# One matmul per partition sum, another order of the first loads, and revised planner estimates, in a fused long-convolution and feed-forward kernel

## The chip, the core and the metric

The kernel runs on one core of a Trainium2 chip. A core has five engines with instruction streams of their own: TensorE (PE in the profile, PEld for its weight loads), VectorE (DVE), ScalarE (ACT), GpSimd (POOL) and SyncE (SP), which here only issues loads and stores. The metric is the device time of one execution in microseconds (us), lower is better; a kernel's time is the median of its runs.

## What is computed

```python
x  = A_q                                  # [1, 2048, 1024]
xn = layernorm(x)                         # over the last axis, eps 1e-5

# A: gated long convolution, channel by channel
k_shift = sum over t of k_pad[:, t:t+S] * shift_k[:, 3-t]     # 4 taps, causal
kv = k_shift * v
y  = irfft(rfft(pad(kv)) * rfft(pad(ssm_k)))[:S] + kv * ssm_D
A  = xn * y

# B: feed-forward, 1024 -> 3584 -> 1024
B  = silu(xn @ w1) @ w2

out = x + A + B
```

The inputs are float32. The kernel splits every operand of its large products into a high and a low float16 part and multiplies high by high, high by low and low by high, so each product of the algorithm is three matmuls. The scale factors for these parts are powers of two, which come from sums of squares over a whole operand.

## The kernel before

**An order written by a planner.** The kernel doesn't issue its instructions in the order of its text. Each piece of work is a generator ("stream") that yields operations (`Op`, line 81) with an engine, an estimated busy time, what is read and written, and a margin. `Order.run` (line 153) keeps a clock for each engine, takes the stream whose next operation could start earliest (less a bias that the stream has set), emits it, and moves the engine's clock on by the estimate. So an estimate doesn't only describe: it decides in which order the instructions of all five engines stand in the program. On the chip each engine then works through its own list in order and waits where data are missing. The estimates are in four helpers: `V` for VectorE (line 232), `A` for ScalarE (235), `T` for TensorE (238) and `L` for loads on SP's queue (241). Nearly all VectorE operations are recorded by lines 250 and 253 (`v_tt`, `v_stt`), nearly all of ScalarE by line 261 (`a_act`), and the loads and stores by line 243, so in the profile one goes by tile names.

**Rows of x.** x has 16 row tiles of 128 x 1024. `load_row` (370) loads one into a ring of four buffers, `xt`. `ln_rows` (376) takes rows in pairs: statistics on VectorE (`bn_stats`, two halves, line 394) or, for two later pairs, on ScalarE; a square root on ScalarE; a chain of six short VectorE instructions (410 to 415); and the normed row (426), written to a ring of eight buffers, `xn`. `transposes` (433) turns normed rows into column order on TensorE (line 447), through three PSUM tiles `ft`. `first_rows` (455) splits rows 0 to 3 into the operands A11 and A12; `x_rows` (518) makes the sums and differences of a Strassen-Winograd scheme for the rest.

**The first GEMM.** w1 is taken in 14 pairs of 128-column blocks. `load_pair` (579) loads one: the first two in four pieces each (tiles named `x` in the trace, whose space they borrow), the others in two pieces (`raw`). `scales_w1` (600) squares the pieces on ScalarE with a running total for each piece and partition, sums them with `norm`, and derives the scale; `factors_w1` (636) splits the blocks into the tiles `wo`. `feed_forward` (804) first computes four plain units (pairs 0 and 1 by rows 0 to 3, then by rows 4 to 7), then 12 units of seven products for the first half of the rows and 14 for the second; lines 748 to 750 are their matmuls. `evacuate` and `block` turn the results into hidden tiles `ht` (a ring of four) and store them to memory (`hs`).

**The sum over partitions.** `norm` (336) has columns of partial sums in `ss`, in one or two groups of `ns` columns. A product with a 128 x 128 matrix of ones puts the sum over all partitions into every partition: one matmul for each column, accumulated over a group's columns (line 349). Then a chain on VectorE rounds to a power of two (332, 333) and computes scales (618 to 622 for w1). `norm` is called 14 times for w1 (4 columns for the first two pairs, 2 for the others), and for each of the 8 channel groups of the convolution twice: in `gate` with 4 + 2 columns and in `result_scales` with 4; once more for w2 with one.

**The convolution and the second GEMM.** For each of 8 groups of 128 channels: the taps and the product with v on ScalarE and VectorE (`gate`, 988), transposes (1045), a first transform stage by matmuls with constants (1072 to 1074, tiles `ps`), butterflies and the complex product on VectorE (`forward`, `product`, `inverse`), a split into `zh` and `zl`, the inverse stage by matmuls (1276 to 1278, tiles `py`), and the gate with xn, `yt`, which is added to the output by DMAs on GpSimd's queue (247; two `yt` buffers). Between these stand the products of the first GEMM and, from about the middle of the run on, those of the second: `feed_forward` loads hidden tiles into `wo` and multiplies them by the split w2 (832 to 834), for 2 column halves x 16 row tiles x 28 blocks x 3 parts, 2688 matmuls. Their streams have a bias of zero, so they fill what the convolution leaves.

**The start.** `begin` (1313) issues row 0, the first w1 pair, rows 1 to 3 and the second pair; then `more_rows` and `more_pairs` go on side by side. The convolution's constants (`taps`, `cfw`, `civ`) follow the fourth pair's place in `more_pairs`. Line 1342 loads ScalarE's square-root table ahead of everything.

Of the kernel before, what the change touches and what calls it, by code (L numbers as in the profile page):

```python
# [17 lines left out]
AX = mybir.AxisListType  # L18
# [189 lines left out]
def h3_ffn_kernel(ctx, tc, x, kp, vs, fs, shift, dskip, w1, w2, cfwd, cinv, out):  # L208
# [26 lines left out]
    def A(f, o, ins, us=None, m=0.15):  # L235
        return Op("ACT", us or 1.03 * (0.12 + size(o) * 0.98e-3), 0.2, f, ins, [o], m)
# [19 lines left out]
    def a_act(o, i, func, scale=1.0, bias=None, total=None):  # L256
# [61 lines left out]
    xts_r = Ring(order, lnp, "xt", 4)  # L318
    xns_r = Ring(order, lnp, "xn", 8)
# [16 lines left out]
    def norm(ring, ss, ns, then, flags):  # L336
# [6 lines left out]
        cols = len(ns)  # L343

        def mm():
            for c, n in enumerate(ns):
                for a in range(n):
                    i = sum(ns[:c]) + a
                    nc.tensor.matmul(pt[:, c:c + 1], ones, ss[:, i:i + 1], start=(a == 0), stop=(a == n - 1))
# [20 lines left out]
    def load_row(t):  # L370
        yield xts_r.ready
        xts[t] = xts_r.tile([P, D])
# [3 lines left out]
    def ln_rows():  # L376
        for t0, n, on_act, bias in ((0, 2, 0, 0.2), (2, 2, 0, 0.17), (4, 2, 0, 0.13), (6, 2, 0, 0.12),
# [5 lines left out]
            for t in range(t0, t0 + n):  # L383
# [4 lines left out]
                else:  # L388
# [3 lines left out]
                    def stats(st=st, ag=ag, xt=xt, i=i):  # L392
                        for a in range(2):
                            nc.vector.bn_stats(st[:, a, :], xt[:, a * W:(a + 1) * W])
# [3 lines left out]
                    p = V(stats, m[:, 0, i], [xt], us=1.5)  # L398
# [17 lines left out]
            p = V(chain, rstd[:, q], [m[:, 3, :], m[:, 4, :], m[:, 0, :]], us=0.6)  # L416
            p.writes += [nmr[:, q], m[:, 5, :]]
            yield p
            for t in range(t0, t0 + n):
                yield xns_r.ready  # L420
                xns[t] = xns_r.tile([P, D], uses=4 if t < 4 else 2)
                xn, xt, i = xns[t][0], xts[t][0], slice(t - t0, t - t0 + 1)
                if on_act:
                    yield a_act(xn, xt, AF.Identity, rstd[:, t:t + 1], nmr[:, t:t + 1])
                else:
                    yield V(lambda: nc.vector.tensor_scalar(xn, xt, m[:, 0, i], rstd[:, t:t + 1], op0=ADD, op1=MUL),
# [970 lines left out]
```

## Time and profile before

| what | us |
|---|---|
| median of 3 runs | 1356.01 |
| lowest and highest run | 1355.55, 1360.4 |
| the profiled execution | 1360.99 |
| its span | 1358.9 |
| TensorE busy in it | 1301.7 |
| VectorE busy | 1184.0 |
| ScalarE busy | 689.2 |
| GpSimd busy | 99.4 |

The span runs from the first to the last instruction that the profiler saw. Busy time is the union of an engine's instructions. TensorE's matmuls are pipelined: a 128 x 512 matmul is shown with some 0.38 us, but the next one starts 0.215 us after it, so the distance of two starts is the cost of one, and a TensorE that is shown as busy is not for that reason at its full rate. In rows of the timeline the columns are start, duration, engine, line, operation, tiles written and read, shape and count, and in brackets the idle time before, with what ended it. In rows by line the numbers behind the bar are busy us and mean ns of one, and behind the next bar the idle time before them. In a table of stretches each engine has its busy time and, in brackets, its number of instructions, and the last three columns are the granted clock, the busy share of the DMA engines and GB/s.

### The profile page before, as it was taken

Reading aid. Unit: us, or ns where it says so; the run is one execution under the profiler, and the core shown is the slowest. Engines: PE = TensorE matmul, PEld = TensorE weight load, DVE = VectorE, ACT = ScalarE, POOL = GpSimd, SP = SyncE. Lnnn points to the kernel's source line nnn. Section 1 sums busy time; section 2 is a strip of 40 time slices with the busy share of each in tenths; the row PEclk is TensorE's granted clock in tenths of the full one; section 3 lists DMA queues with packets and bytes.
Section 4 is the critical chain, followed back from the end, with each engine's and each line's share of the span. In section 5 each row is a group of like instructions: output and inputs, shape, how many; then the busy total and the mean of one; then the engine's idle time right before and its main releaser. Section 6 shows DMA issues by size and latency. Waiting matters only on the chain.

```text
span 1358.9 us, 18422 instructions
## 1 busy us (share of the span) xinstructions
PE 1301.7 (96%) x6394; PEld 642.1 (47%) x6394; DVE 1184.0 (87%) x1856; ACT 689.2 (51%) x1211; POOL 99.4 (7%) x102
## 2 busy tenths in 40 slices
PE   6899999999999989999899999999999999999998
PEld 5544454444444444444444544545544454454443
DVE  6987999889899968999989999999999999999600
ACT  6879787878567665546533433423473252341200
POOL 0000000000000011000120120120110020021110
PEclk9899999999999998999999999999999999999999
DMA  8257588989899887758775485575596366355461
GB/s 310 78 168 228 185 286 292 328 286 394 289 315 328 280 249 200 227 156 261 214 173 157 112 197 148 122 187 143 124 292 177 97 150 185 91 125 127 112 128 16
DMA packets 206861, 269.69 MB, mean 198 GB/s; under 512 B 15400, under 2 KB 121904, under 8 KB 204336
## 3 DMA queue, kind: packets, MB, share of 16 engines
q1 hardware_dynamic: 184752, 251.73, 58.1%
q0 software_dynamic: 22016, 16.78, 10.2%
q8 instruction: 50, 0.82, 0.2%
q14 instruction: 43, 0.35, 0.1%
HBM read 192.96 MB, written 83.89 MB: 204 GB/s over the span
## 4 chain that ended last, share of the span: by engine, by line
PE 33%; issue 25%; DVE 22%; DMA 11%; ACT 5%; POOL 3%; SPq 0%; POOLq 0%; DVEq 0%; ACTq 0%
PE ff L750 8%; PE ff L749 8%; PE ff L748 8%; DVE spec L250 6%; POOL out L247 3%; DMA out<-yt 3%; DMA raw<-in_w 2%; DVE acc L253 2%; DMA kin<-in_kp 2%; DVE tmp L250 2%; PE ff L833 2%; PE ff L834 2%; PE ff L832 2%; DVE wo L253 1%; DVE x L253 1%
## 5 line engine op out<-in xcount | busy, mean ns | idle before, releaser
L833 PE MATMUL ff<-x,wo 128*128 128x512 f16 x896 | 342.3, 382 | 4.8 <-DVE x L253 4.8
L834 PE MATMUL ff<-x,wo 128*128 128x512 f16 x896 | 342.3, 382 | 0.0
L832 PE MATMUL ff<-x,wo 128*128 128x512 f16 x896 | 341.8, 381 | 0.0
L748 PE MATMUL ff<-x,wo 128*128 128x512 f16 (+1 forms) x808 | 306.4, 379 | 2.3 <-ACT wo L261 2.3
L750 PE MATMUL ff<-x,wo 128*128 128x512 f16 (+1 forms) x808 | 305.9, 379 | 2.1 <-DVE wo L253 2.1
L749 PE MATMUL ff<-x,wo 128*128 128x512 f16 (+1 forms) x808 | 305.7, 378 | 0.6 <-DVE x L253 0.6
L250 DVE TENSOR_TENSOR spec<-spec 128x512 f32<-128x512 f32 (+2 forms) x192 | 219.7, 1174 | 1.3
L834 PEld LDWEIGHTS <-wo 128*128 128x128 f16 x896 | 88.2, 98 | 112.9 <-issue 8.8
L832 PEld LDWEIGHTS <-wo 128*128 128x128 f16 x896 | 89.0, 99 | 100.8 <-issue 2.2
L833 PEld LDWEIGHTS <-wo 128*128 128x128 f16 x896 | 88.1, 98 | 101.2 <-issue 2.4
L750 PEld LDWEIGHTS <-wo 128*128 128x128 f16 x808 | 79.8, 99 | 98.9 <-DVE wo L253 4.7
L247 POOL DMA_DIRECT2D out<-yt x64 | 70.5, 1102 | 752.4 <-DMA w2n<-in_w 484.5
L748 PEld LDWEIGHTS <-wo 128*128 128x128 f16 x808 | 81.4, 101 | 89.7 <-ACT wo L261 2.5
L749 PEld LDWEIGHTS <-wo 128*128 128x128 f16 x808 | 80.0, 99 | 88.5 <-issue 1.9
L250 DVE TENSOR_TENSOR tmp<-spec 128x512 f32<-128x512 f32 (+1 forms) x112 | 100.7, 917 | 0.3
L253 DVE SCALAR_TENSOR_TENSOR ht<-hf,wsc,ht 128x512 f16<-128x512 f32 x112 | 83.2, 746 | 8.5 <-ACT ht L261 8.2
L261 ACT ACTIVATE xg<-xg,nmr,rstd 128x128 f32<-128x128 f32 x128 | 55.1, 484 | 65.9 <-DMA xg<-in_x 54.2
L261 ACT ACTIVATE ht<-hf,wsc 128x512 f16<-128x512 f32 x112 | 80.8, 721 | 3.4
L253 DVE SCALAR_TENSOR_TENSOR acc<-kin,taps,acc 128x512 f32<-128x512 f32 x96 | 71.7, 747 | 8.7 <-ACT acc L261 8.6
L261 ACT ACTIVATE hf<-hf,wsc 128x512 f32<-128x512 f32 x78 | 55.8, 715 | 40.5 <-DVE hf L250 40.4
L261 ACT ACTIVATE kin<-acc 128x512 f32<-128x512 f32 x32 | 20.1, 627 | 102.3 <-DVE acc L250 102.2
L261 ACT ACTIVATE v<-ff,invc 128x512 f32<-128x512 f32 x32 | 21.7, 677 | 94.3 <-PE ff L834 94.2
(152 smaller groups left out, 1834.9 us busy)
## 6 DMA issues: line engine op xcount, KB each, us to landing
wo<-hs SPq DMA_DIRECT2D x224, 256.0 KB, 3.1
hs<-ht SPq DMA_DIRECT2D x112, 256.0 KB, 3.8
ws<-wo SPq DMA_DIRECT2D x84, 256.0 KB, 4.6
wo<-ws SPq DMA_DIRECT2D x84, 256.0 KB, 4.2
w2n<-in_w SPq DMA_DIRECT2D x80, 256.0 KB, 5.4
raw<-in_w SPq DMA_DIRECT2D x28, 512.0 KB, 6.0
kin<-in_kp SPq DMA_DIRECT2D x32, 448.0 KB, 3.7
xt<-in_x SPq DMA_DIRECT2D x16, 512.0 KB, 4.8
```

Source lines behind the costliest of these rows:

```text
L247: return Op("POOL", 1.1, 4.0, lambda: nc.gpsimd.dma_start(o, i, accum_op=ADD), [i], [o], m, n)
L250: return V(lambda: nc.vector.tensor_tensor(o, a, b, op=op), o, [a, b], **k)
L253: return V(lambda: nc.vector.scalar_tensor_tensor(o, a, s, b, op0=op0, op1=op1), o, [a, b] + ([] if isinstance(s, float) else [s]), **k)
L261: nc.scalar.activation(o, i, func, scale=scale, **kw)
L748: nc.tensor.matmul(o, w[:, 0, k], xf[:, :, k, 0], start=first and k == 0, stop=False, **kw)
L749: nc.tensor.matmul(o, w[:, 0, k], xf[:, :, k, 1], start=False, stop=False, **kw)
L750: nc.tensor.matmul(o, w[:, 1, k], xf[:, :, k, 0], start=False, stop=last and k == KH - 1, **kw)
L832: nc.tensor.matmul(po, hx[:, jj, 0, :], wc[:, jj, 0, :], start=(j == 0), stop=False)
L833: nc.tensor.matmul(po, hx[:, jj, 0, :], wc[:, jj, 1, :], start=False, stop=False)
L834: nc.tensor.matmul(po, hx[:, jj, 1, :], wc[:, jj, 0, :], start=False, stop=(j == NF - 1))
```

## The change

```diff
     def A(f, o, ins, us=None, m=0.15):
-        return Op("ACT", us or 1.03 * (0.12 + size(o) * 0.98e-3), 0.2, f, ins, [o], m)
+        return Op("ACT", us or 1.02 * (0.16 + size(o) * 0.84e-3), 0.2, f, ins, [o], m)
...
-        return Op("SP", 0.07, 0.1, lambda: nc.sync.dma_start(o, i), [i], [o], m, n)
+        return Op("SP", 0.4, 0.1, lambda: nc.sync.dma_start(o, i), [i], [o], m, n)
...
         p = A(f, o, ins)
+        p.busy += 0.07 * (len(ins) - 1) - 0.06 * (i.space == bass.MemoryType.PSUM)
...
-    xts_r = Ring(order, lnp, "xt", 4)
-    xns_r = Ring(order, lnp, "xn", 8)
+    xts_r = Ring(order, lnp, "xt", 12)
...
-        cols = len(ns)
+        cols, n = len(ns), sum(ns)
 
         def mm():
-            for c, n in enumerate(ns):
-                for a in range(n):
-                    i = sum(ns[:c]) + a
-                    nc.tensor.matmul(pt[:, c:c + 1], ones, ss[:, i:i + 1], start=(a == 0), stop=(a == n - 1))
-
-        outs = []
+            nc.tensor.matmul(pt[:, 0:n], ones, ss, start=True, stop=True)
 
         def chain():
-            pow2(e[:, 0:cols], pt[:, 0:cols])
+            for c, m in enumerate(ns):
+                q = sum(ns[:c])
+                if m > 1:
+                    nc.vector.tensor_reduce(e[:, c:c + 1], pt[:, q:q + m], axis=AX.X, op=ADD)
+                else:
+                    nc.vector.tensor_copy(e[:, c:c + 1], pt[:, q:q + 1])
+            pow2(e[:, 0:cols], e[:, 0:cols])
             then(e[:, 0:cols])
 
-        yield T(mm, pt[:, 0:2], [ss], 0.12 * sum(ns), m=0.5)
-        p = V(chain, e, [pt[:, 0:2]], us=0.6)
+        yield T(mm, pt[:, 0:n], [ss], 0.25, m=0.5)
+        p = V(chain, e, [pt[:, 0:n]], us=1.1)
...
-        xts[t] = xts_r.tile([P, D])
+        xts[t] = xns[t] = xts_r.tile([P, D], uses=4 if t < 4 else 2)
...
-            p = V(chain, rstd[:, q], [m[:, 3, :], m[:, 4, :], m[:, 0, :]], us=0.6)
+            p = V(chain, rstd[:, q], [m[:, 3, :], m[:, 4, :], m[:, 0, :]], us=1.05)
...
-                    yield V(lambda: nc.vector.tensor_scalar(xn, xt, m[:, 0, i], rstd[:, t:t + 1], op0=ADD, op1=MUL),
-                            xn, [xt, m[:, 0, i], rstd[:, t:t + 1]], us=0.78)
-                xts[t][1].set()
+                    yield V(lambda: nc.vector.tensor_scalar(xt, xt, m[:, 0, i], rstd[:, t:t + 1], op0=ADD, op1=MUL),
+                            xt, [xt, m[:, 0, i], rstd[:, t:t + 1]], us=0.78)
...
-                        yield T(mm, po, [hx[:, jj], wc[:, jj]], 3 * (W / 2400 + 0.003))
+                        yield T(mm, po, [hx[:, jj], wc[:, jj]], 3 * 0.2185)
...
     def begin():
-        yield from load_row(0)
+        for t in (0, 1):
+            yield from load_row(t)
         yield from load_pair(0)
-        for t in range(1, 4):
+        for t in (2, 3):
             yield from load_row(t)
         yield from load_pair(1)
+        for t in range(4, 8):
+            yield from load_row(t)
         add(more_rows(), 0.05)
         add(more_pairs(), 0.05)
 
     def more_rows():
-        for t in (4, 5, 6, 7):
-            yield from load_row(t)
         for t in (8, 9, 12, 13, 10, 11, 14, 15):
             yield from load_row(t)
+        yield L(taps, shift)
+        yield L(cfw, cfwd)
+        yield L(civ, cinv)
...
+    def warm_up():
+
+        pt, tok = ft.tile([P, KH, P])
+        for _ in range(22):
+            yield T(lambda: nc.tensor.matmul(pt[:, 0, :], ones, ones, start=True, stop=True), pt[:, 0, :], [], 0.44)
+        tok.set()
...
     add(begin(), 0.05)
+    add(warm_up(), 0.0)
```

There are five parts. The first: `norm` puts all columns through one matmul and adds a group's columns afterwards with a reduction on VectorE (a copy where a group has one column). The second: rows 0 and 1 are loaded ahead of the first w1 pair, rows 4 to 7 directly behind the second pair, and the convolution's constants behind the last rows. The third: a row is normed in place, in a ring of 12 buffers in place of 4 + 8; a buffer comes free when the row's transposes are done. The fourth: 22 matmuls of the matrix of ones with itself stand at the head of TensorE's order; their result isn't read. The fifth: estimates and biases of the planner have other values: ScalarE's formula with terms for operands and PSUM, 0.4 for a load's issue on SP (also in `copies`, line 864), 1.1 and 1.05 for the two VectorE chains, 0.5 for a set of transposes, 0.2185 for a second-GEMM matmul. The statistics of a row, one operation of 1.5 in the planner's eyes, are now three (two of 0.65 and one of 0.5). The biases of the first streams (rows, scales and factors of w1) are raised by a few hundredths.

More of the change, by code (lines that the diff above doesn't have):

```diff
@@ L376, in ln_rows @@
     def ln_rows():
[L377 removed]
+        for t0, n, on_act, bias in ((0, 2, 0, 0.26), (2, 2, 0, 0.17), (4, 2, 0, 0.13), (6, 2, 0, 0.12),
                                      (8, 2, 1, 0.03), (12, 2, 1, 0.03), (10, 2, 0, 0.03), (14, 2, 0, 0.03)):
@@ L390, in ln_rows, with moments @@
                     ag = lnp.tile([P, 2], F32, name="ag", bufs=2)
-                    def stats(st=st, ag=ag, xt=xt, i=i):
-                        for a in range(2):
-                            nc.vector.bn_stats(st[:, a, :], xt[:, a * W:(a + 1) * W])
+                    for a in range(2):
+                        yield V(lambda: nc.vector.bn_stats(st[:, a, :], xt[:, a * W:(a + 1) * W]), st[:, a, :],
+                                [xt[:, a * W:(a + 1) * W]], us=0.65)
+                    def moments():
                         nc.vector.bn_aggr(ag, st)
```

21 lines of the change are left out of this document (9 added, 12 removed).

## The prediction

> **What bounds the kernel now.** I read the page first, then a table of stretches, then the end of the timeline, because an average of 96% on one engine and 87% on another doesn't say which of the two ends the run.
>
> ```profile
> PE 1301.7 (96%) x6394; PEld 642.1 (47%) x6394; DVE 1184.0 (87%) x1856; ACT 689.2 (51%) x1211; POOL 99.4 (7%) x102
> PE   6899999999999989999899999999999999999998
> DVE  6987999889899968999989999999999999999600
> ...
> 0.00:60.00 60.00, 41.22 (x238) 29.83 (x239) 46.67 (x129) 43.49 (x79) 0.69 (x6) 0.95 0.63 220
> 60.00:250.00 190.00, 185.98 (x907) 91.06 (x907) 173.83 (x350) 153.55 (x245) 0.00 (x0) 0.99 0.71 227
> 250.00:500.00 250.00, 244.65 (x1185) 117.34 (x1183) 227.75 (x356) 179.17 (x346) 3.44 (x3) 0.99 0.94 312
> 500.00:700.00 200.00, 187.81 (x890) 88.49 (x888) 179.28 (x258) 104.17 (x175) 15.62 (x15) 0.97 0.73 207
> 700.00:1290.00 590.00, 579.92 (x2893) 287.35 (x2892) 555.62 (x764) 206.08 (x363) 70.61 (x70) 0.99 0.60 151
> 1290.00:1359.00 69.00, 62.17 (x289) 27.99 (x286) 0.88 (x2) 2.75 (x4) 9.01 (x9) 0.97 0.36 71
> ```
>
> After the width of a stretch come the busy times of PE, PEld, DVE, ACT and POOL. Four stages are to be seen. Up to 60 us PE is idle for 18.8 us: the start is fed by VectorE. From 60 to 500 PE is the fuller one. From 700 to 1290 both are nearly full, 580 and 556 of 590 us: VectorE carries the long convolution, and PE fills the time between with feed-forward products. From 1290 VectorE has nothing left, and PE works off what remains. So two chains are almost level, and the end shows how they stand:
>
> ```profile
> 1284.08 0.38 PE L834 MATMUL ff<-x,wo 128*128 128x512 f16 x1
> 1287.23 0.28 PE L1276 MATMUL py<-zh,civ 128*128 128x256 f16 x1 [2.78 <-DVE yt L253]
> ...
> 1288.56 0.38 PE L832 MATMUL ff<-x,wo 128*128 128x512 f16 x1
> 1288.77 0.38 PE L833 MATMUL ff<-x,wo 128*128 128x512 f16 x1
> ...
> 1351.80 0.38 PE L834 MATMUL ff<-x,wo 128*128 128x512 f16 x1
> ...
> 1286.30 0.88 DVE L253 SCALAR_TENSOR_TENSOR yt<-py,csc,xg 128x256 f32<-128x256 f32 x2 [5.18 <-DMA out<-yt]
> ```
>
> The last inverse-transform product waits 2.78 us for VectorE; behind it stand 294 second-GEMM products in PE's order, one each 0.215 us, which is the 63.4 us from 1288.56 to the end of 1351.80; then 6.7 us of copy-out follow. The time is therefore "when VectorE lets the last inverse transform through" plus "products left behind it". A saving on PE counts only in so far as the order moves products from behind that point to ahead of it.
>
> **The change part by part.** *One matmul for each sum.* Today a sum over partitions is one product per column:
>
> ```profile
> 316.66 1.40 PE L349 MATMUL px<-css,ones 128*128 128x1 f32 x12
> 317.92 0.38 PE L748 MATMUL ff<-x,wo 128*128 128x512 f16 x1
> ...
> L349 PE MATMUL px<-css,ones x160: 167/250/271, 316.7 to 1258.2; 128*128 128x1 f32 x160
> L349 PE MATMUL nm<-ss,ones x52: 167/250/373, 6.1 to 226.8; 128*128 128x1 f32 x52
> L349 PE MATMUL px<-ss,ones x12: 167/250/271, 258.1 to 289.6; 128*128 128x1 f32 x12
> L349 PE MATMUL px<-q,ones x2: 167/208/250, 523.6 to 523.6; 128*128 128x1 f32 x2
> ```
>
> The six products of a convolution group are twelve instructions, two passes each, and hold PE from 316.66 to 317.92, so 1.26/12 = 0.105 us a pass. There are 160+52+12+2 = 226 passes. Afterwards each of 31 sums (14 for w1, 16 for the groups, one for w2) is one product of two passes: 62. Removed: 164 passes, 17.2 us; 36 of them lie in w1's part, 128 in the convolution. A pass with up to six columns instead of one isn't in the trace; it lies between 0.105 and the 0.11 us of a full 128-column pass (the transposes at full clock in the fence on the start, 1.47 us for twelve, less the last one's run-out), so 62 passes cost at most 0.3 us more. I take none. In the changed program's order 213 second-GEMM products stand behind the last inverse transform instead of 294: 81 x 0.215 = 17.4 us, the same amount seen from the end. Term: -17.2.
>
> *The reductions this moves to VectorE.* 14 + 16 + 8 reductions and one copy are new, 39 instructions on a few columns:
>
> ```profile
> L891 DVE TENSOR_REDUCE q<-q 128x1 f32<-128x14 f32 x1 | 0.2, 168 | 0.0
> L332 DVE TENSOR_SCALAR pow<-px 128x2 f32<-128x2 f32 x8 | 1.3, 160 | 0.5 <-PE px L349 0.5
> ...
> 26.10 0.16 DVE L618 RECIPROCAL wsc<-pow 128x1 f32<-128x1 f32 x1
> 26.30 0.15 DVE L619 TENSOR_SCALAR wsc<-wsc 128x1 f32<-128x1 f32 x1
> ```
>
> One takes 0.16 to 0.17 us, and in a dependent chain the next starts 0.2 us later, so 39 x 0.19 = 7.4 us. The 14 of w1 lie mostly from 60 to 250 us, where VectorE is idle for 16 us and PE sets the pace: nothing, and 2.7 us if that cover is gone. The other 25 stand in the chain of the convolution: +4.7.
>
> *The start.* The rows that set it:
>
> ```profile
> 4.64 1.29 DVE L394 BATCH_NORM_STATS2 st<-xt 128x6 f32<-128x512 f32 x2 [3.63 <-DMA xt<-in_x]
> 9.66 1.29 DVE L394 BATCH_NORM_STATS2 st<-xt 128x6 f32<-128x512 f32 x2 [3.24 <-DMA xt<-in_x]
> 13.37 1.53 DVE L426 TENSOR_SCALAR xn<-xt,mv,rstd 128x1024 f32<-128x1024 f32 x2
> 14.32 2.79 PE L447 MATMUL ft<-ident,xn 128*128 128x128 f32 x12 [4.44 <-DVE xn L426]
> 18.80 0.42 PE L748 MATMUL ff<-x,wo 128*128 128x256 f16 x1
> 25.64 0.42 PE L750 MATMUL ff<-x,wo 128*128 128x256 f16 x1
> 25.85 0.42 PE L748 MATMUL ff<-x,wo 128*128 128x256 f16 x1
> 27.09 0.27 PE L750 MATMUL ff<-x,wo 128*128 128x256 f16 x1
> 27.20 1.47 PE L447 MATMUL ft<-ident,xn 128*128 128x128 f32 x12
> 53.05 1.15 PE L447 MATMUL ft<-ident,xn 128*128 128x128 f32 x8 [2.73 <-DVE xn L426]
> 59.17 1.28 DVE L253 SCALAR_TENSOR_TENSOR x<-ft,x 128x512 f16<-128x512 f32 x2
> ...
> 10.00:20.00 10.00, 4.89 (x22) 4.08 (x23) 9.55 (x31) 6.28 (x14) 0.00 (x0) 1.00 1.09 359
> ```
>
> Row 1 of x comes behind four w1 loads, and VectorE waits 3.24 us for it. With rows 0 and 1 ahead that wait goes, the norm of both starts some 4 us earlier, and the first product can come near 14 instead of 18.80. But the third product unit needs rows 4 to 7 split, the last of them by the row at 59.17, and that is VectorE's work: counted in both orders, the same instructions stand ahead of that point, and in the new one three reductions (0.6 us) and one subtraction of the third w1 pair (0.6) besides. The 3.24 us wait goes, about 1.5 us of short gaps go with rows 4 and 5 in hand earlier, 1.2 us of work come: -3.5. Bounds: 0 (VectorE waits for ScalarE instead) and -6 (all short gaps go as well). Eight further rows (0.52 MB each) stand ahead of the third pair of w1 on SP's queue: its first half lands after 9.4 MB, about 28 us at the 359 GB/s of the last row above; in the new order ScalarE first reads it behind the second pair's splits, near 32: nothing, and up to 3 us on ScalarE, not VectorE, if that cover is gone. Taps and transform constants, later on the queue, are first read by the convolution, past 250 us. Norming in place frees no engine, but a row's buffer is now held until its transposes are done, so the last four row loads wait longer on SP, and the first write of a hidden tile stands behind the third of them. There are four hidden tiles, and only four are filled before the third unit: nothing, and a pause of ScalarE's fifth tile if that is wrong.
>
> *The 22 constant products* run where PE has only sums to do. By the transposes' pass at the early clock, (2.79-0.4)/11 = 0.22 us, two passes each are 9.6 us, at full clock 4.8: from about 1 us they end between 6 and 10.6, and the first sum is due near 10. They cost 0 to 0.6 us and I take 0. What they may bring is the clock: the gap of two equal products is 0.21 us at 25.64 and 0.11 at 27.09, so today the first products ran at half rate. Since VectorE feeds this stage, I give that nothing beyond the start's own term. The Trainium skill's "TensorE: Matmul & The Clock Gate" (Part 1) states that the array starts at half rate, is released after some 3.4 us of sustained work and falls back after as long an idle window; its Part 4 adds that transposes don't count as work. By that rule the constants' effect may be lost again before the first product near 14 us, as PE then does only sums and transposes; the trace agrees that a gap (the 2.73 us before 53.05) is followed by products at half rate. By it the 48 half-width products that stand ahead of rows 2 and 3 in PE's new order would last 48 x 0.21 = 10 us from 14, about 1 us past the time when those rows are ready, and the sum would be -19.0 instead of -20.0.
>
> *The revised estimates* move the order. The planner counted 0.6 us for a norm chain of six or more VectorE instructions, which at the 0.2 us above take 1.2 and more; with 1.05 and 1.1 it now sees VectorE nearer to what the rows show. In the new order the first two groups' inverse transforms stand behind 7 to 14 us more of PE's work, by count. Waits this bears on:
>
> ```profile
> PE ps L1072 <- DVE spec L250: 8.9, 4, 7.4
> PE ff L833 <- DVE x L253: 4.8, 5, 1.7
> ...
> DVE yt L253 <- DMA out<-yt: 26.7, 7, 9.7
> ```
>
> PE's 7.4 us wait came from a transform placed too early for VectorE; more products ahead of it cover it. Bounds: -12.2 (7.4 and the 4.8 of the w2 splits go, and VectorE gets all of it as earlier work) to +10 (VectorE waits for PE as long as PE now leads). As VectorE itself sets the end, only a part comes out: I take -4.
>
> Sum: -17.2 + 4.7 - 3.5 - 4 = -20.0. The profiled execution took 1360.99 us with a span of 1358.9, so 1341 for its like; it stood 5 us above the median of 1356.01, so the median comes to 1336.
>
> **The rivals.** *Everything comes out* (chance 0.17): start -6, waits -12.2, and the 4.7 us of reductions fall into VectorE's gaps, of which 700 to 1290 has 34 us: -17.2 - 6 - 12.2 = -35.4, 1321. For it: PE's own work falls by all of 17.2 us, and 13.7 us of its waits stand in the rows above. Against: VectorE is then fuller than it has ever been here.
>
> *VectorE eats the saving* (0.18): all 7.4 us of reductions land on its chain, the start gives nothing, and the new order makes VectorE wait 4 us more: -17.2 + 7.4 + 4 = -5.8, 1350. For it: 556 of 590 us busy, and the 2.78 us wait at the end. Against: the fewer products behind the last transform are in the program whatever VectorE does.
>
> *The writes of the result hold VectorE* (0.07): two yt buffers go out by adding DMAs, and VectorE waited for them 7 times, 26.7 us, 3.8 us each. If the order, which in two of eight groups now bunches twelve inverse products where they stood in sixes, makes it wait twice a group, 16 times, that is 9 x 3.8 = 34 us more on the chain that sets the end: +14, 1370. It turns slower by over 0.5% from seven more waits on. Against: in six groups the spacing is the same, and so are the buffers.
>
> *The sums cost nothing today* because PE waits there anyway (0.03): then the products behind the last transform would be reached no earlier, and only the start is left: 1352.
>
> **How the numbers follow.** My forecast has 0.55, with its own range 1328 to 1345. Within 0.5%, 6.8 us, is about what can't be told from no change; faster ends at 1349. Faster: 0.55 + 0.17 + half of 0.18 = 0.81. Same: the other half and the 0.03, 0.12. Slower: 0.07. The range reaches down to the first rival and up into the second: 1321 to 1353.
>
> **What would show it.** Right: 62 sum passes in place of 226; first product before 15 us; the third unit's last split by 57; about 46 us of products alone at the end; VectorE done between 1285 and 1295. Wrong: a VectorE end after 1305, a first product that waits for the constants, over ten waits for out<-yt, or new PE waits of over 10 us between 250 and 700.

## The result, and the profile after

| | before | changed |
|---|---|---|
| median, us | 1358.05 (4 runs, 1355.55 to 1360.4) | 1343.53 (4 runs, 1341.59 to 1344.91) |
| span of the profiled execution, us | 1358.9 | 1342.3 |
| last inverse-transform product starts, us | 1288.45 | 1289.46 |
| second-GEMM products behind it | 294 | 213 |
| VectorE busy / idle up to 1290 us | 1183.1 / 106.9 | 1189.9 / 100.1 |

The ratio of the changed kernel to the one before is 0.9892, with a 95% interval from 0.9866 to 0.9919: 14.5 us by the medians. The span is 16.6 us shorter.

The page of the changed kernel, with the busy time of each engine and the span in 40 slices:

```profile
span 1342.3 us, 18219 instructions
...
PE 1283.7 (96%) x6274; PEld 623.2 (46%) x6274; DVE 1190.8 (89%) x1895; ACT 686.9 (51%) x1211; POOL 99.3 (7%) x102
...
PE   6799999998999999998999999999999999999998
...
DVE  8887899987899997999999999989989999999920
```

TensorE does 18.0 us less, VectorE 6.8 us more. VectorE's last work ahead of the final products ends at 1288.2 us, 54 us before the end, where it was 1287.2 and 72. The same table of stretches as before (PE, PEld, DVE, ACT, POOL busy, then granted clock, DMA share, GB/s):

```profile
0.00:60.00 60.00, 41.43 (x273) 31.17 (x274) 49.60 (x136) 44.62 (x82) 0.70 (x6) 0.98 0.68 231
60.00:250.00 190.00, 185.86 (x905) 89.46 (x904) 172.42 (x361) 153.35 (x244) 0.00 (x0) 1.00 0.68 221
250.00:500.00 250.00, 241.86 (x1139) 112.31 (x1138) 224.99 (x350) 170.95 (x326) 2.41 (x3) 0.99 0.90 307
500.00:700.00 200.00, 196.00 (x939) 92.31 (x938) 186.89 (x272) 110.67 (x196) 18.02 (x17) 0.99 0.80 227
700.00:1290.00 590.00, 572.86 (x2814) 277.40 (x2812) 556.04 (x778) 205.29 (x362) 70.05 (x69) 0.99 0.60 151
1290.00:1343.00 53.00, 45.71 (x212) 20.58 (x210) 0.88 (x2) 2.06 (x3) 8.15 (x8) 0.98 0.33 53
```

Take each stretch's width less VectorE's busy time and compare with before. VectorE's idle time goes from 13.3 to 10.4 us in the start, from 16.2 to 17.6 and from 22.3 to 25.0 in the next two, from 20.7 to 13.1 between 500 and 700, and stays at 34.0 after 34.4 from there to 1290. So the start's gain is there at 60 us, is given back by 500, and comes once more between 500 and 700; all together VectorE idles 6.8 us less up to 1290 us and works 6.8 us longer in the same time. TensorE's timeline shows what that means for the end:

```profile
1286.39 0.38 PE L836 MATMUL ff<-x,wo 128*128 128x512 f16 x1
1288.25 0.28 PE L1278 MATMUL py<-zh,civ 128*128 128x256 f16 x1 [1.48 <-DVE yt L253]
...
1289.46 0.27 PE L1280 MATMUL py<-zh,civ 128*128 128x256 f16 x1
1289.57 0.38 PE L834 MATMUL ff<-x,wo 128*128 128x512 f16 x1
...
1335.33 0.38 PE L836 MATMUL ff<-x,wo 128*128 128x512 f16 x1
```

The last inverse transform again waits for VectorE and comes at the same time as before, 1289.46 against 1288.45. What changed is the work behind it: 45.9 us of products where 63.4 us stood. TensorE got rid of 17.2 us of sums and did 81 products more ahead of that point, in the same time. The sums themselves, by line and form:

```profile
L346 PE MATMUL px<-css,ones x32: 169/252/378, 329.8 to 1260.6; 128*128 128x6 f32 x16, 128*128 128x4 f32 x16
L346 PE MATMUL nm<-ss,ones x24: 167/251/273, 10.3 to 243.5; 128*128 128x2 f32 x20, 128*128 128x4 f32 x4
L346 PE MATMUL px<-ss,ones x4: 168/251/272, 266.4 to 282.5; 128*128 128x2 f32 x4
```

These are 60 passes, and w2's sum has two more: 62 for 226. VectorE's waits that the prediction watched:

```profile
DVE ht L253 <- ACT ht L261: 15.2, 12, 3.3
DVE yt L253 <- DMA out<-yt: 11.6, 4, 7.5
```

VectorE waits for the writes of the result 4 times, 11.6 us, against 7 times and 26.7 us before; but a second profile of the changed kernel (after_again, below) has 7 such waits and 17.3 us, so the number of them isn't settled by one profile. Waits for ScalarE's hidden tiles are longer in both (15.2 and 14.7 us against 8.2).

### The profile page after: what moved, and what is told of

It reads as the page before. It is cut to its first block, busy times and chain, and to the rows that moved or that the text cites. A ratio compares the mean times of both kernels' runs of the same rounds, so it can differ in the third digit from the quotient of the medians.

```text
span 1342.3 us, 18219 instructions
## 1 busy us (share of the span) xinstructions
PE 1283.7 (96%) x6274; PEld 623.2 (46%) x6274; DVE 1190.8 (89%) x1895; ACT 686.9 (51%) x1211; POOL 99.3 (7%) x102
## 3 DMA queue, kind: packets, MB, share of 16 engines
q0 software_dynamic: 22016, 16.78, 10.4%
## 4 chain that ended last, share of the span: by engine, by line
PE 35%; DVE 22%; issue 21%; DMA 12%; ACT 8%; POOL 2%; POOLq 0%; SPq 0%; DVEq 0%; ACTq 0%
PE ff L752 7%; PE ff L751 7%; PE ff L750 7%; DVE spec L250 6%; PE ff L835 3%; PE ff L834 3%; PE ff L836 3%; DVE tmp L250 3%; DMA w2n<-in_w 2%; DVE acc L253 2%; POOL out L247 2%; DMA out<-yt 2%; DMA kin<-in_kp 2%; DVE wo L253 1%; ACT hf L261 1%
## 5 line engine op out<-in xcount | busy, mean ns | idle before, releaser
L253 DVE SCALAR_TENSOR_TENSOR ht<-hf,wsc,ht 128x512 f16<-128x512 f32 x112 | 83.0, 746 | 15.6 <-ACT ht L261 15.2
L261 ACT ACTIVATE v<-ff,invc 128x512 f32<-128x512 f32 x32 | 21.8, 682 | 100.3 <-PE ff L836 100.2
L261 ACT ACTIVATE zh<-spec,csc 128x1024 f16<-128x1024 f32 x32 | 36.0, 1141 | 66.0 <-DVE spec L253 53.5
```

Of the source, the lines that this page charges most:

```text
L253: return V(lambda: nc.vector.scalar_tensor_tensor(o, a, s, b, op0=op0, op1=op1), o, [a, b] + ([] if isinstance(s, float) else [s]), **k)
L261: nc.scalar.activation(o, i, func, scale=scale, **kw)
```

## The experiments

A rule of the prediction makes them easy to read: the end is the start of the last inverse-transform product, plus 0.2157 us for each product behind it, plus some 7 us. It held in every profile within 0.6 us (for the changed kernel: 1289.5 + 213 x 0.2157 + 7.0 = 1342.4, measured 1342.3). So every kernel is described by two numbers, the time of that point and the products behind it, and beside them stands its ratio to the kernel before on the same chip.

| kernel | last inverse product, us | products behind | span, us | ratio, 95% interval |
|---|---|---|---|---|
| before | 1288.5 | 294 | 1358.9 | 1 |
| changed | 1289.5 | 213 | 1342.3 | 0.9892 [0.9866, 0.9919] |
| b_sums_same_order | 1283.3 | 294 | 1353.7 | 0.9966 [0.9947, 0.9986] |
| a_columns_same_order | 1300.5 | 213 | 1353.4 | 0.9952 [0.9926, 0.9977] |
| a_reduce_twice | 1294.6 | 213 | 1347.4 | 0.9922 [0.9893, 0.9951] |
| a_no_constants | 1291.0 | 213 | 1343.8 | 0.9895 [0.9861, 0.9929] |
| after_again | 1286.7 | 213 | 1339.4 | 0.9887 [0.9838, 0.9935] |
| b_sums_planned | 1305.8 | 189 | 1353.5 | 0.9955 [0.9931, 0.9979] |
| a_old_formulas | 1291.9 | 180 | 1337.7 | 0.9848 [0.9792, 0.9904] |
| a_old_loads | 1295.6 | 213 | 1348.4 | 0.9885 [0.9832, 0.9938] |
| b_sums_row_figures | 1309.9 | 189 | 1357.5 | 0.9957 [0.9935, 0.9979] |
| b_sums_figures_in_place | 1286.3 | 180 | 1332.1 | 0.9815 [0.9784, 0.9846] |
| a_old_formulas_again | 1291.4 | 180 | 1337.7 | 0.9826 [0.9806, 0.9846] |
| a_old_formulas_0210 | 1313.2 | 102 | 1342.2 | 0.9869 [0.9847, 0.9891] |

The changed kernel alone, profiled twice, had that point at 1289.5 and at 1286.7, and the single runs of one kernel lie 3 to 16 us apart. So a difference of a few us between two profiles isn't read by itself; the ratio, which rests on several runs, decides. The kernel before had medians of 1361.14 (25 runs), 1359.37 (13) and 1361.62 (17) beside the three groups of experiments.

**The merged sums in the order of before** (b_sums_same_order). The planner is told the old figures, so no other instruction moves. The reductions on VectorE come with it, as in the change.

```diff
-            for c, n in enumerate(ns):
-                for a in range(n):
-                    i = sum(ns[:c]) + a
-                    nc.tensor.matmul(pt[:, c:c + 1], ones, ss[:, i:i + 1], start=(a == 0), stop=(a == n - 1))
+            nc.tensor.matmul(pt[:, 0:n], ones, ss, start=True, stop=True)
...
         yield T(mm, pt[:, 0:2], [ss], 0.12 * sum(ns), m=0.5)
         p = V(chain, e, [pt[:, 0:2]], us=0.6)
```

> The kernel before, with only the sums in one matmul each and the reductions on VectorE; the planner is given the old figures, so every engine keeps the order of before and 294 second-GEMM products stay behind the last inverse transform. Theory one (the end is the moment when VectorE lets the last inverse transform through, plus the products behind it): TensorE's 17.2 us of freed time turn into waits, VectorE carries 7.4 us more, and the time goes up by 0 to 7, 1358 to 1365. Theory two (TensorE's work sets the time wherever it lies): 17 less, 1341. In between, by about 8, if both chains share it.

Measured: 0.9966, 4.6 us of gain, neither the loss of theory one nor the 17 us of theory two; the case in between was put at about 8. The tail is untouched at 294 products; the whole gain is the transform, 5.1 us earlier. Where the other 12 us of freed TensorE time went shows in the sums of the two tables of stretches up to 1280 us, of before:

```profile
sum 1280.00, PE 1232.35 PEld 609.78 DVE 1181.14 ACT 683.36 POOL 88.17; mean PE 246.47 PEld 121.96 DVE 236.23 ACT 136.67 POOL 17.63
```

and of this kernel:

```profile
sum 1280.00, PE 1215.85 PEld 588.80 DVE 1185.42 ACT 684.65 POOL 89.25; mean PE 243.17 PEld 117.76 DVE 237.08 ACT 136.93 POOL 17.85
```

TensorE is busy 16.5 us less in the same 1280 us: it mostly waits longer. Ahead of the last inverse transform VectorE idles 97.0 us where it idled 105.3, and is busy 3.2 us longer: so, by these two profiles, 8.3 of the 17.2 us come off VectorE's waits, and the reductions take 3.2 of them back. TensorE's long wait for the transform stage (7.4 us before) stays as well, as it must when nothing is moved:

```profile
PE ps L1073 <- DVE spec L250: 10.9, 8, 6.4
```

**One column at a time in the order of the changed kernel** (a_columns_same_order), the opposite cut: the reductions go, the 164 passes come back, the planner still sees 0.25 and 1.1.

```diff
-            nc.tensor.matmul(pt[:, 0:n], ones, ss, start=True, stop=True)
+            for c, n in enumerate(ns):
+                for a in range(n):
+                    i = sum(ns[:c]) + a
+                    nc.tensor.matmul(pt[:, c:c + 1], ones, ss[:, i:i + 1], start=(a == 0), stop=(a == n - 1))
...
-            pow2(e[:, 0:cols], e[:, 0:cols])
+            pow2(e[:, 0:cols], pt[:, 0:cols])
```

> The changed kernel with its order kept, but each sum by columns again: 226 passes instead of 62, no reductions. Theory one: TensorE's 17.2 us more lie in places where it waits for VectorE, VectorE has 7 us less, 213 products stay behind the last inverse transform: 1338 to 1348, about the changed kernel's 1343.5. Theory two: 17 more, 1360.

Measured: 0.9952. In the timeline of this kernel the tail is the same 213 products, but it begins 11 us later:

```profile
1300.53 0.27 PE L1279 MATMUL py<-zh,civ 128*128 128x256 f16 x1
1300.64 0.38 PE L833 MATMUL ff<-x,wo 128*128 128x512 f16 x1
```

That is between the theories: by the ratios 8 us more than the changed kernel, where theory one allowed 5 and theory two asked for 17. In the profiles 17.2 us of TensorE work cost 11 us at the transform, although VectorE is busy 4.2 us less: ahead of that point it idles 114.8 us in place of 99.5. So in this order, with 81 more products placed ahead, some 15 of the 17.2 us reach VectorE, where 8.3 did in the order of before. The merged sums are worth 0.9952 - 0.9892 = 0.0060 of the time here, 8 us, and 4.6 us there.

**Each reduction twice** (a_reduce_twice), which sizes the price on VectorE.

```diff
                 if m > 1:
-                    nc.vector.tensor_reduce(e[:, c:c + 1], pt[:, q:q + m], axis=AX.X, op=ADD)
+                    for _ in range(2):
+                        nc.vector.tensor_reduce(e[:, c:c + 1], pt[:, q:q + m], axis=AX.X, op=ADD)
```

> The changed kernel with its order kept and every reduction issued twice: 38 more short VectorE instructions, 7.2 us, 4.6 of them in the convolution. Theory one: 4 to 7 more, 1348 to 1350. Theory two: nothing, 1343.5, since TensorE's work is the same.

Measured: 0.9922, 0.003 (4 us) above the changed kernel, which is the expected size, but the intervals of the two ratios overlap. The transform comes 5.1 us after the one in the changed kernel's first profile and 7.9 us after the one in its second. VectorE is busy 5.4 us longer than in either, and its idle time ahead of the transform (99.3 us) is that of the first (99.5). So a price of about 5 us fits everything and isn't proved. The reductions in the changed kernel, by line:

```profile
L352 DVE TENSOR_REDUCE pow<-px x26: 148/154/163, 267.3 to 1261.4; 128x1 f32<-128x4 f32 x16, 128x1 f32<-128x2 f32 x10
```

One takes 0.15 us, and the 12 that stand under another tile's name for w1's sums take as long.

**No constant products** (a_no_constants): the 22 operations stay in the planner's order and emit nothing.

```diff
-            yield T(lambda: nc.tensor.matmul(pt[:, 0, :], ones, ones, start=True, stop=True), pt[:, 0, :], [], 0.44)
+            yield T(lambda: None, pt[:, 0, :], [], 0.44)
```

> The changed kernel with its order kept, without the 22 constant products. If the start is fed by VectorE: 0 to 1.5 us more, 1343.5 to 1345, with the first products at half rate (0.21 us apart) until near 22 us. If the clock of the first products sets the start: 4 us more, 1347.5. If the constants delay the first sum: up to 1 us less.

Measured: 0.9895 against 0.9892, no difference. TensorE's timeline without them:

```profile
10.62 2.79 PE L447 MATMUL ft<-ident,xt 128*128 128x128 f32 x12
...
14.49 0.42 PE L750 MATMUL ff<-x,wo 128*128 128x256 f16 x1
...
19.87 0.32 PE L751 MATMUL ff<-x,wo 128*128 128x256 f16 x1
20.02 0.27 PE L752 MATMUL ff<-x,wo 128*128 128x256 f16 x1
```

The products are 0.21 us apart until 19.9 us and 0.11 from there. With the constants they are 0.11 apart from the first in the changed kernel's first profile, and 0.21 apart until 17.8 us in its second, so what the constants bring isn't certain (see the last section). Nothing of it reaches the end: the ratio is the same without them.

**The changed kernel again** (after_again).

> The changed kernel itself, on the chip and with the runs of before of the next three: 0.989 of before, last inverse transform near 1289.5 us of the span, 213 products behind it.

Measured: 0.9887, as at first. The engines have the same instructions in the same order as in the first profile, and the last inverse transform comes 2.8 us earlier.

**The merged sums, planned with their new figures** (b_sums_planned): the kernel before with the change's first part alone, and the planner free to move the rest.

```diff
-        yield T(mm, pt[:, 0:2], [ss], 0.12 * sum(ns), m=0.5)
-        p = V(chain, e, [pt[:, 0:2]], us=0.6)
+        yield T(mm, pt[:, 0:n], [ss], 0.25, m=0.5)
+        p = V(chain, e, [pt[:, 0:n]], us=1.1)
```

> The kernel before with the sums in one matmul each and their new figures (0.25 and 1.1), so the planner makes a new order; old loads, no constants, old formulas. 189 products stand behind the last inverse transform instead of 294, 22.6 us less. Theory one (the gain of the change is this shift): the transform goes near 1285 to 1290 as in the same order, and the time is 15 to 22 less than before, at least as good as the whole change. Theory three (the rest of the change is needed): the transform goes later by as much as stands ahead of it, and the gain is under 8.

Measured: 0.9955, 6 us of gain where the theory that the shift gives the gain asked for 15 to 22. The planner now leaves 189 products at the end, 22.6 us less than before, but the transform is 17 us later (and 22.6 us later than in b_sums_same_order, which has the same instructions in the order of before):

```profile
1305.84 0.27 PE L1279 MATMUL py<-zh,civ 128*128 128x256 f16 x1
1305.95 0.38 PE L833 MATMUL ff<-x,wo 128*128 128x512 f16 x1
```

Fewer products behind the point aren't a gain of their own: TensorE does them ahead of it, and the convolution may wait for that.

**Old formulas in the changed kernel** (a_old_formulas): ScalarE's formula without its new terms, a load's issue and the second GEMM as before; the figures for the two VectorE chains, the statistics and the transposes stay new.

```diff
-        return Op("ACT", us or 1.02 * (0.16 + size(o) * 0.84e-3), 0.2, f, ins, [o], m)
+        return Op("ACT", us or 1.03 * (0.12 + size(o) * 0.98e-3), 0.2, f, ins, [o], m)
...
-        return Op("SP", 0.4, 0.1, lambda: nc.sync.dma_start(o, i), [i], [o], m, n)
+        return Op("SP", 0.07, 0.1, lambda: nc.sync.dma_start(o, i), [i], [o], m, n)
...
-        p.busy += 0.07 * (len(ins) - 1) - 0.06 * (i.space == bass.MemoryType.PSUM)
...
-                        yield T(mm, po, [hx[:, jj], wc[:, jj]], 3 * 0.2185)
+                        yield T(mm, po, [hx[:, jj], wc[:, jj]], 3 * (W / 2400 + 0.003))
...
```

> The changed kernel with the old figures for ScalarE, for loads and for the second GEMM (chains, sums, loads order, constants as changed). 180 products stand behind the last transform instead of 213, 7.1 us less. If the revised figures bring nothing: the transform goes as late as in the changed kernel and the time is 4 to 7 less, 1337 to 1340. If they make the plan truer: waits of over 7 us come back between 300 and 700 us, the transform goes 8 or more later, and the time is 1345 to 1352.

Measured: 0.9848, and when it was run again (a_old_formulas_again) 0.9826 with a tighter interval, 0.9806 to 0.9846, wholly below the changed kernel's first one of 0.9866 to 0.9919 (its second, 0.9838 to 0.9935, was wider and overlaps by a little). The revised formulas bring nothing. In the one group of runs that has both kernels, 0.9887 - 0.9848 makes them cost 5 us, with overlapping intervals; 0.9892 - 0.9826, from two groups, makes it 9. By the spans of the four profiles it is 2 to 5. The sign is the surer part.

> The changed kernel with the old figures for ScalarE, loads and second GEMM once more: 0.985 of before, transform near 1292, 180 products behind it.

**The old order of the first loads** (a_old_loads): `begin`, `more_rows` and `more_pairs` as before.

```diff
     def begin():
-        for t in (0, 1):
-            yield from load_row(t)
+        yield from load_row(0)
         yield from load_pair(0)
-        for t in (2, 3):
+        for t in range(1, 4):
             yield from load_row(t)
...
```

> The changed kernel with the first loads in the old order (row 0, first w1 pair, rows 1 to 3, second pair), everything else as changed, planned anew; 213 products stay behind the last transform. If the start's 3 us reach the end: 3 to 4 more, 1347. If PE's fill from 60 to 500 us swallows them: no difference, 1343.5. The first product comes near 18 us in either case.

Measured: 0.9885 against 0.9887, with single runs from 1340.6 to 1350.4 us. The first product of the timeline is late again, and so is the third unit's last split, at 60.44 us on VectorE:

```profile
18.69 0.42 PE L750 MATMUL ff<-x,wo 128*128 128x256 f16 x1
```

4.3 us at the first product and 3.1 us at the third unit are worth nothing that the time shows. The profiled execution was one of the longer ones, with its transform 6 to 9 us after the changed kernel's, and the medians don't bear that difference out.

**The ladder's next two steps** started from b_sums_planned. b_sums_row_figures adds the finer statistics of a row and the new figures for the norm chain and the transposes; b_sums_figures_in_place adds to that the rows normed in place in a ring of 12, and nothing else.

```diff
...
-                    p = V(stats, m[:, 0, i], [xt], us=1.5)
+                    p = V(moments, m[:, 0, i], [st], us=0.5)
...
-            p = V(chain, rstd[:, q], [m[:, 3, :], m[:, 4, :], m[:, 0, :]], us=0.6)
+            p = V(chain, rstd[:, q], [m[:, 3, :], m[:, 4, :], m[:, 0, :]], us=1.05)
...
-            yield T(mm, pt, [xn], 0.45, m=0.3)
+            yield T(mm, pt, [xn], 0.5, m=0.3)
```

> The kernel before with merged sums, planned anew, and the changed figures for the rows' norming (statistics as three operations, 1.05 for the chain, 0.5 for transposes); 189 products behind the last transform. If truer figures for VectorE are what the merged sums lacked: the transform goes near 1292 instead of 1306, ratio 0.985 to 0.988. If not: as merged sums alone, 0.995 to 0.998, transform at 1302 or later.

```diff
-    xts_r = Ring(order, lnp, "xt", 4)
-    xns_r = Ring(order, lnp, "xn", 8)
+    xts_r = Ring(order, lnp, "xt", 12)
...
-        xts[t] = xts_r.tile([P, D])
+        xts[t] = xns[t] = xts_r.tile([P, D], uses=4 if t < 4 else 2)
...
-                yield xns_r.ready
-                xns[t] = xns_r.tile([P, D], uses=4 if t < 4 else 2)
...
```

> As the run before this one, and rows normed in place in a ring of 12; old loads, no constants, old biases; 180 products behind the last transform, the same as in the changed kernel with the old formulas (0.985). If the ring is what was lacking: 0.983 to 0.988, transform near 1292. If what is left (biases of the first streams, constants, loads) is needed: 0.992 or more.

Measured: the row figures change nothing (0.9957 after 0.9955). The ring, on top of them, brings the ratio to 0.9815: 0.0142, or 19 us, from one edit, and a kernel that beats both, with a median of 1337.8 against 1361.62 for before on its chip. (The two spans differ by 25 us, because one profiled execution was 3 us above its kernel's median and the other 4 us below.) The stretches of b_sums_row_figures from 500 us on:

```profile
500.00:700.00 200.00, 186.67 (x887) 87.48 (x885) 177.14 (x261) 105.79 (x186) 15.40 (x15) 0.98 0.76 211
700.00:1290.00 590.00, 569.23 (x2774) 273.71 (x2772) 550.65 (x770) 197.48 (x352) 68.61 (x68) 0.99 0.59 150
```

and of b_sums_figures_in_place:

```profile
500.00:700.00 200.00, 194.57 (x953) 93.47 (x951) 187.13 (x275) 110.32 (x190) 18.04 (x18) 1.00 0.78 215
700.00:1290.00 590.00, 580.09 (x2872) 281.68 (x2870) 558.59 (x781) 207.43 (x364) 72.86 (x72) 1.00 0.61 153
```

VectorE idles 22.9 us of the first stretch without the ring and 12.9 with it, 39.4 and 31.4 of the second; TensorE is busier by 7.9 and 10.9 us. VectorE norms its last row at 170 us without the ring and at 177 with it, and the gain lies behind 500 us. TensorE, VectorE and ScalarE have the same instructions in both, as many of each kind, in another order, which the planner wrote with the other buffers. So this is no engine's saved work. What the worse order waited for stands in VectorE's waits from 500 to 1290 us, without the ring:

```profile
DVE acc L253 <- ACT acc L261: 13.8, 12, 1.7
DVE yt L253 <- DMA out<-yt: 10.4, 4, 5.8
DVE yt L253 <- DMA xg<-in_x: 6.1, 1, 6.1
...
DVE yt L253 <- DMA w2n<-in_w: 3.8, 1, 3.8
```

and with it:

```profile
DVE yt L253 <- DMA out<-yt: 14.4, 7, 3.9
DVE acc L253 <- ACT acc L261: 5.2, 10, 1.0
```

Waits for ScalarE's `acc` fall by 8.6 us, and single waits of 6.1 and 3.8 us for transfers go. That looks like many positions that fit better rather than one cause, but no run shows it. Nor do the runs show that the ring is good for the order as such: it wasn't tried with other figures, and another small edit of the planner's inputs may move the time as far (the next one moves the transform by 21.8 us).

**The second GEMM's figure** (a_old_formulas_0210), to see what pulling more products ahead does: a_old_formulas with 0.2100 us for a second-GEMM matmul, which the planner takes as room for more of them.

```diff
-                        yield T(mm, po, [hx[:, jj], wc[:, jj]], 3 * (W / 2400 + 0.003))
+                        yield T(mm, po, [hx[:, jj], wc[:, jj]], 3 * 0.2100)
```

> The same with 0.2100 for a second-GEMM product: 102 products behind the last transform instead of 180, 16.8 us less, so 16.8 more ahead of it. If VectorE alone sets the transform's time: 16.8 less, 1323. By what the columns in the changed order showed (11 of 17 us ahead of it came out as delay): the transform some 10 us later, and 5 to 8 less, 1333 to 1336. If VectorE now waits for TensorE one for one: no gain.

Measured: 0.9869 against 0.9826. Only 102 products stay behind, 78 fewer (16.8 us), and the transform comes 21.8 us later: more than all of it is given back, which is beyond even the last of the three cases expected. The stretches of this kernel from 700 us on:

```profile
700.00:900.00 200.00, 197.19 (x967) 95.98 (x965) 182.00 (x262) 67.85 (x122) 21.92 (x22) 0.98 0.58 148
900.00:1100.00 200.00, 196.17 (x935) 92.59 (x934) 191.33 (x268) 73.07 (x128) 20.85 (x21) 0.98 0.66 172
1100.00:1280.00 180.00, 173.80 (x851) 84.16 (x850) 163.43 (x221) 55.11 (x103) 24.59 (x24) 0.98 0.55 132
```

VectorE idles 18.0, 8.7 and 16.6 us in them; in a_old_formulas_again it is 8.0, 6.7 and 7.7. Past a point the filler holds the convolution up by more than its own length.

## Why the prediction was right, and where it was not

**The sign and the rule of the end were right.** Faster by 14.5 us, inside the range, 7.5 us above the forecast of 1336. The rule "when VectorE lets the last inverse transform through, plus the products behind it" gives the span of all 14 profiles from the measured time of that point. Of the signs that were named, the 62 passes, the first product before 15 us, the 46 us of products at the end and VectorE's end at 1288 us came true. The third unit's last split was to come by 57 us and came at 57.30.

**The conversion to the median was off.** The profile of before stood 5 us above the median of three runs, and the forecast took 5 us off. With 13 to 25 runs, on other occasions, the kernel before had medians of 1359 to 1362, so its profiled execution of 1360.99 had been an ordinary one. The changed kernel's profiled execution took 1344.26, against 1341 forecast: 3.3 of the 7.5 us are the terms, the rest is this step.

**The sums' -17.2 was mis-sized.** Counts held: 62 passes, 81 products fewer behind the transform, 45.9 us of products at the end. But the step took the whole TensorE time for gain and charged only VectorE's 4.7 against it, -12.5 in all. Alone, in the order of before, the pair is worth -4.6 us, planned anew -6, and in the changed kernel's order -8; much of what was freed became waits of TensorE. The prediction had said itself that a saving on TensorE counts only as the order moves products ahead; it then treated that move as free. b_sums_planned and a_old_formulas_0210 show its price: 22.6 us moved for 22.6 us of delay against b_sums_same_order, and 16.8 for 21.8 against a_old_formulas_again.

**The reductions' +4.7 fits what was measured**: 0.15 us each, some 5 us at the transform for a second set, though within the noise of the ratios.

**The start's -3.5 was about half there in its own place and nothing at the end.** First product at 14.36 us, the third unit's last split at 57.30 (59.17 before, so 1.9 us), VectorE idle 2.9 us less at 60 us. It was given back by 500 us, and with the old load order the time is the same. A gain in an early stage that the order doesn't carry to the handoff at the end isn't a term of the sum.

**The constants' 0 held**: 0.9895 without them. The doubt that the clock may be lost again before the first product was right in the second profile and not in the first, and the ratio is the same in both.

**Norming in place, "nothing", failed most.** The step asked which engine and which buffer it would hold up, and there the answer holds: no pause is to be seen. But it put the term at nothing without counting the ring as an input to the planner. In the ladder it is the largest part of all, 0.9957 to 0.9815.

**The revised estimates' -4 had the wrong sign for the formulas.** They cost some 5 us (0.9848 and 0.9826 without them), and the figures of the chains and statistics are worth nothing (0.9957 after 0.9955). TensorE's 7.4 us wait did go, but not for the reason that the step gave. The longest of its kind is 1.1 us in the changed kernel; with the new figures of chains and statistics alone (b_sums_row_figures) it is still 5.2, with the ring on top of them (b_sums_figures_in_place) 1.0, and without the new formulas (a_old_formulas) 2.4. The first three of these, in this order:

```profile
PE ps L1074 <- DVE spec L250: 2.6, 5, 1.1
PE ps L1075 <- DVE spec L250: 7.7, 5, 5.2
PE ps L1071 <- DVE spec L250: 2.1, 4, 1.0
```

So it went with the order that the ring gave, and not with the figures.

By the ratios, and across chips, the ladder adds up: about -6 for the merged sums, planned; 0 for the row figures; -19 for the ring; between 0 and +5 for loads, biases and constants (0.9826 and 0.9848 after 0.9815); +5 to +9 for the formulas; together -11 to -20, where 14.5 was measured. The forecast of -20 came near because a term that it missed (-19) and terms that it oversized or gave the wrong sign point in opposite ways: that the number came so near is luck. Each step's worth depends on the order it is added to, as the two values of the merged sums show, so this is one path through the parts and not the only one.

**The rivals.** "VectorE eats the saving" (1350) was right that the start gives nothing at the end, but it charged 7.4 us for the reductions, where some 5 is what the runs bear out, and 4 us of new waits, where VectorE's idle time fell by 6.8 us. "Everything comes out" (1321) failed: neither the start nor the whole of the sums reached the end. "The writes of the result hold VectorE" asked for nine more waits; there were 4 and 7 in the two profiles, against 7. "The sums cost nothing" (1352) fails in the order of before, where the sums alone bring the last transform 5.1 us forward.

What stays open: why the planner's order with the ring of 12 is the better one. The runs show that it is and where VectorE waits less, not which position does it, nor whether another new order would have done as well.

## What to carry to other kernels

Where two chains are level and a planner writes the order, price a change as two numbers, the time of the last handoff between the chains and the work left behind it; filler pulled ahead of the handoff pays only until the other chain waits for it (22.6 us moved for 22.6 us of delay, and 16.8 for 21.8, in two orders here). Give the planner the old figures for a new instruction (or emit nothing for an old one): that separates what the instruction costs from what the new order does. An edit that only changes buffers or figures is not "nothing" there: it is a new order, and its worth is found by running it.

## What the runs showed of the hardware

**The constants don't make the clock at the start certain.** TensorE's timeline at the start of the changed kernel, first profile:

```profile
1.06 7.69 PE L1344 MATMUL ft<-ones 128*128 128x128 f32 x44 [1.06 <-DVE ones L294]
10.31 0.39 PE L346 MATMUL nm<-ss,ones 128*128 128x4 f32 x2 [1.56 <-ACT junk L261]
10.90 1.50 PE L447 MATMUL ft<-ident,xt 128*128 128x128 f32 x12 [0.20 <-DVE xt L427]
...
14.36 0.27 PE L750 MATMUL ff<-x,wo 128*128 128x256 f16 x1
```

Twelve transposes take 1.50 us (2.79 without the constants) and the products behind them are 0.11 us apart: the full rate was kept from the constants' end at 8.75 us to the first product. In the second profile of the same program (after_again) it wasn't. The transposes from 10.46 us on take 2.23 us, and the products are 0.21 apart until 17.8 us. The granted clock, the third number from the end, fell to half in between:

```profile
4.24:11.07 6.83, 4.50 (x39) 4.25 (x39) 5.79 (x19) 2.92 (x9) 0.00 (x0) 1.00 1.04 382
11.07:17.89 6.82, 5.55 (x27) 4.03 (x25) 6.61 (x19) 6.59 (x15) 0.00 (x0) 0.50 1.06 389
```

In the clock records of all 14 profiles two changes stand whole multiples of 3.41 us apart (6.83 is two of them), and where the first one falls differs from profile to profile: 6.36 us in the first profile of the changed kernel, 4.24 in the second. That fits one program keeping its clock in one execution and losing it in the next; no run shows that it is the cause.

**Transposes can raise the clock.** In b_sums_same_order, which has no constants, TensorE does two sum passes at 9.03 us and then nothing but transposes up to the first product:

```profile
9.03 0.59 PE L346 MATMUL nm<-ss,ones 128*128 128x4 f32 x2 [9.03 <-ACT junk L261]
14.26 2.79 PE L448 MATMUL ft<-ident,xn 128*128 128x128 f32 x12 [4.65 <-DVE xn L427]
17.84 0.66 PE L448 MATMUL ft<-ident,xn 128*128 128x128 f32 x4 [0.79 <-DVE x L253]
18.34 0.27 PE L749 MATMUL ff<-x,wo 128*128 128x256 f16 x1
```

The first twelve run at half rate (0.22 us each), the last four at full rate (0.11), and the clock records have the rise at 17.52 us. The Trainium skill's "TensorE: Matmul & The Clock Gate", Part 4, says that transposes don't count as work for the clock; here, for float32 ones, they did, and b_sums_row_figures has the same at 18.0 us. They don't always: without the constants (a_no_constants) the transposes from 10.62 us on raised nothing, and the clock rose near 19.9 us, 5.4 us after the first product.

**Merging columns is nearly free on TensorE.** Where it runs without a wait, the two passes of a sum hold it for 0.14 us by the distance of starts, with the one column of w2's sum as with two, four or six columns (one sum of two columns took 0.24 us, one of six 0.29); twelve passes of one column took 1.26 us.
